# Loads of w_in and w_out issued by GpSimd instead of SyncE, in an attention and gated-MLP kernel on one core

## Chip, cores and metric

One Trainium2 chip, one of its cores. The metric is the device time of one execution of the kernel, in microseconds (us). The profile is one further execution, recorded by the hardware profiler.

## What is computed

An attention over 8 batches, 12 heads, 448 positions and 64 features, with a normalization of q and k, then a gated MLP with a residual. Cut to what matters:

```python
q_n, k_n = rmsnorm(q, g_q), rmsnorm(k, g_k)            # q, k, v: (8, 12, 448, 64) float32
scores = 1 / sqrt(64) * matmul(q_n, k_n.T)
attn = exp(scores - max(scores)); attn = attn / (sum(attn) + 1e-9)
x = matmul(attn, v)                                    # rearranged to (8, 448, 768)
h = gelu(x @ w_in)                                     # w_in: (768, 1024)
u, v = h[..., :512], h[..., 512:]
v_n = (v - mean(v)) / sqrt(var(v) + 1e-6) * g_ln
gated = u * (einsum('ts,bsd->btd', w_sg, v_n) + b_sg)  # w_sg: (448, 448)
return x + gated @ w_out                               # w_out: (512, 768)
```

`w_in` and `w_out` are stored as 64-bit floats. The kernel loads their raw words and builds 32-bit floats from them.

## The kernel before

**Two programs in one.** The text of the kernel writes down the work with engines bound to a `Tape` instead of the hardware: each call becomes a `Task` with an engine, a cost and a priority (its place in the text plus an offset). `Tape.schedule` then simulates the five engines and SyncE's DMA queue with the costs of `Tape.cost`, takes for each free engine the ready task of the best priority, and `Tape.emit` sends the instructions out in the order of the simulated begins. So the order on each engine is fixed when the kernel is built, and an engine runs its instructions in that order, each waiting for what it needs. All instructions sent by `emit` carry the line L439 in the profile, so groups are told apart by the names of tiles.

**The attention.** A unit is one pair of head pairs (24 units in all). For each, `load_qk` loads q and k into `qk`, `squares` and `norms` find the norms (`sqk`, `ss`, `nx`, `ny`), and `split` multiplies them in (on GpSimd, but for unit 0), cuts the result into two 16-bit halves `hl` and transposes these by DMA into `qt`. `scores` runs seven steps: matmuls `s`, a running minimum on VectorE (`jk`), the exponential on ScalarE (`ex`), a split into halves (`ahl`, on VectorE or ScalarE) and a DMA transpose into `at`. `pv` multiplies by v, takes reciprocals of the sums (`recips`, partly on GpSimd: `rx`, `rh`, `rl`) and writes the halves `xh` and `xl`.

**The weights.** `weights` is a generator that runs beside the first twelve steps of the attention. `load_raw` (L602 on) loads w_in in 12 pieces of 128 rows by 1024 words (`raw`, three buffers, `RAWB`); `decode` turns each into floats in five VectorE instructions (`dec`), and then ScalarE and VectorE write the two 16-bit parts `wi`. Further on come w_sg (`wsr`), transposed by DMA into `ws_h` and `ws_l`, and w_out in 8 pieces (`rawo`, L673 on), decoded the same way into `wr`. A piece's buffer is free for the next load when VectorE has read the last word of the piece in it. The first piece (`RAWF` = 1) may go at once; the others are held in the plan (`tape.after`) until the transposes of the first unit are out.

**Queues.** Every DMA, loads, stores and transposes alike, is issued by SyncE, in one queue, in the order of the plan. The plan models this queue: `schedule` keeps the time when the queue is empty, and the end of each SyncE DMA follows from it. A DMA on another engine has a fixed cost in the plan: `cost` returns 700 ns of issue and 4000 ns until the data is there.

**GpSimd and VectorE.** `Tape.port` says which tasks use the port to the on-chip memory that the two engines share: every GpSimd task, and VectorE's elementwise ones between tiles outside PSUM. The plan keeps them apart, and `emit` lets a GpSimd task of more than `LONG` (500 ns) wait for the VectorE port task sent before it.

**The MLP.** `moe` runs once per batch, interleaved with the attention of the next batches; its matmuls need the decoded weights.

Of the kernel before, what the change touches and what calls it, by code (L numbers as in the profile page):

```python
# [8 lines left out]
F32 = mybir.dt.float32  # L9
# [6 lines left out]
ALU = mybir.AluOpType  # L16
# [28 lines left out]
NQK, NVR, RAWB = 2, 2, 3  # L45
NAT, NAH, NQT, NVH, HLB, GV = 2, 3, 2, 4, 3, 3
NOT, NX, NEX = 2, 6, 2
EXP_SET = "natural_log_exp_and_others"
BACC_KW = dict(dynamic_dma_scratch_size=1024)
TILE_KW = dict()  # L50
# [53 lines left out]
class Tape:  # L104
# [30 lines left out]
    def cost(self, q, op, a, kw):  # L135

        aps = [x for x in kw.values() if isinstance(x, bass.AP)]
        n = max([self.free(x) for x in aps], default=1)
        wide = [k for k in ("in_", "in0", "in1") if k in kw and self.free(kw[k]) > max(n // 2, 1)]
        psum = any(self.tiles[kw[k].tensor.name].pool.space for k in wide if kw[k].tensor.name in self.tiles)  # L140
        if q.eng == "T":
            t, big = kw["lhsT"], kw["rhs"]
            rows, cols = (64 if ap_n <= 64 else 128 for ap_n in (t.shape[0], self.free(t)))
            m = self.free(big)
            d = max(m / 2.4, 26.7 if cols == 64 else 53)
            if big.dtype == F32R:
                d = max(d, 186)
            if big.dtype == F32:
                d = max(4 * m / 2.4, 250)
            return d * rows * cols / 128 ** 2 + (4 if rows == cols == 128 else 3), 170, (rows, cols)  # L150
        if q.eng != "S" and "dma" in op:
            return 700, 4000, None
        if q.eng == "S":
            b = n * kw["out"].shape[0] * mybir.dt.size(kw["out"].dtype)
            if "transpose" in op:
                return 1530, b / 458752, True
            return 600, b / 220e3, False
        if "preload" in op:
            return 1283, 0, None
        if q.eng == "A":  # L160
            ptr = sum(isinstance(kw.get(k), bass.AP) for k in ("bias", "scale"))
            return 0.833 * n + (52 if psum else 95) + 85 * ptr + (CA if "accum_out" in kw else 0), 100, None
        if q.eng == "V":
            if op == "reciprocal":
                return 70 + 6.5 * n, 75, None
            ptr = sum(isinstance(kw.get(k), bass.AP) for k in ("scalar", "scalar1", "scalar2"))
            one = len(wide) == 1 and not psum and "reduce" not in op and "bn" not in op and "accum_out" not in kw
            f32 = one and (mybir.dt.size(kw[wide[0]].dtype) == 4 or kw[wide[0]].dtype == U16)
            return (0.52 if f32 else 1.04) * n + 70 + 50 * ptr + (CV if "accum_out" in kw else 0), 85, None
        if n < 100:  # L170
            return 1.5 * n + 185, 20, None
        wide = [k for k in wide if len([x for x in kw[k].ap if x[0]]) == len(kw[k].ap)]
        return (1.86 if len(wide) > 1 else 2.5 if op == "tensor_scalar" else 1.64) * n + 210, 20, None
# [27 lines left out]
    def record(self, q, op, a, kw):  # L201
# [9 lines left out]
            t.id, t.off, t.key = len(self.tasks), self.off, key  # L211
            self.tasks.append(t)
        self.count += 1
        if q.eng == "S":
            t.preds |= self.after
        self.last = t if pe else None
        t.calls.append((q, op, a, kw))
# [229 lines left out]
def kernel(  # L447
# [74 lines left out]
    T, A, V, G, SP = (Queue(tape, e, x) for e, x in zip("TAVGS", (nc.tensor, nc.scalar, nc.vector, nc.gpsimd, nc.sync)))  # L522
    mm = T.matmul
    ENG = dict(A=A, V=V, G=G)

    def copy(out, in_, on):
        tape.either(*[(ENG[e], *(("activation", dict(out=out, in_=in_, func=AF.Copy)) if e == "A" else
# [9 lines left out]

    def two(out, in0, in1, op, on):
        tape.either(*[(ENG[e], "tensor_tensor", dict(out=out, in0=in0, in1=in1, op=op)) for e in on])

    SSW = 2 * C7

# [37 lines left out]
    def decode(dst, raw, most=None):  # L580

        hi, lo = raw[:, :, 1], raw[:, :, 0]
        di = dst.bitcast(I32)
        V.tensor_scalar(out=di, in0=hi, scalar1=0x7FFFFFFF, scalar2=None, op0=ALU.bitwise_and)
        more = {} if most is None else dict(op1=ALU.max, accum_out=most)
        V.tensor_scalar(out=dst, in0=dst, scalar1=LEAST, scalar2=None, op0=ALU.max, **more)
        V.tensor_scalar(out=di, in0=di, scalar1=3, scalar2=0x3FFFFFF8, op0=ALU.logical_shift_left, op1=ALU.bitwise_and)
        V.scalar_tensor_tensor(out=di, in0=hi, scalar=-0x40000000, in1=di, op0=ALU.bitwise_and, op1=ALU.bitwise_or)
        V.scalar_tensor_tensor(out=di, in0=lo, scalar=29, in1=di, op0=ALU.logical_shift_right, op1=ALU.bitwise_or)

    def weights():
        wi = const.tile([P, KT, 2, 2, DH], F16, name="wi")
# [9 lines left out]
        def load_raw(j):  # L602
            if j < len(chunks):
                x, t = chunks[j]
                held, tape.after = tape.after, set() if j < RAWF else tape.after
                raws[j] = stage.tile([P, DH, 2], I32, name="raw", bufs=RAWB)
                SP.dma_start(out=raws[j].rearrange("p a b -> p (a b)"),
                             in_=wi_b[t * P:(t + 1) * P, x * 2 * DH:(x + 1) * 2 * DH])
                tape.after = held

# [2 lines left out]
        for x in (1, 0):  # L613
# [13 lines left out]
            for t in range(KT):  # L627
                wh, wl = (wi[:, t, x, n] for n in range(2))
                A.activation(out=wh, in_=dec[t], func=AF.Copy, scale=wsc)
                V.scalar_tensor_tensor(out=wl, in0=dec[t], scalar=wsc, in1=wh, op0=ALU.mult, op1=ALU.subtract)  # L630
                if t % 2:
                    yield
            W["h", x], W["l", x] = wi[:, :, x, 0], wi[:, :, x, 1]
# [5 lines left out]

        wsr = [mlp.tile([P, S], F32, name="wsr", tag="ug", bufs=5) for c in range(CK)]  # L640
        for s_ in range(C7):
            SP.dma_start(out=wsr[s_ // 2][s_ % 2 * HP:(s_ % 2 + 1) * HP],
                              in_=w_sg.rearrange("(p c) s -> c p s", c=C7)[s_])
        spart = const.tile([P, CK], F32, name="ws_part")
        G.memset(out=spart, constant=0.0)
# [25 lines left out]
        for j in range(2 * FT):  # L671
            t, es = j // 2, slice(j % 2 * EH, (j % 2 + 1) * EH)
            raw = mlp.tile([P, EH, 2], I32, name="rawo", tag="v" + "hl"[j % 2])  # L673
            SP.dma_start(out=raw.rearrange("p a b -> p (a b)"),
                         in_=wo_b[t * P:(t + 1) * P, 2 * EH * (j % 2):2 * EH * (j % 2 + 1)])
            wr = mlp.tile([P, EH], F32, name="wr", tag="gt", bufs=NOT)
            decode(wr, raw)
# [22 lines left out]
    def load_qk(u, qs=None):  # L700
        if u >= NI // NG:
            return
        qs = qs or [SP]
        b, h0 = u // NU, u % NU * 2 * NG
        qk = ld.tile([P, 2, 2, C7, D], F32, name="qk", bufs=NQK)
        for x, src in enumerate((q, k)):
# [8 lines left out]
    def load_v(i):  # L715
# [7 lines left out]
        vp = vr.rearrange("p g c d -> p g (c d)")  # L723
        src = v[b, 2 * g:2 * (g + GV)].rearrange("(g h) (p c) d -> h p g (c d)", h=2, c=C7)
        for h, half, s0, c0, n in ((0, lo, 0, 0, C4), (0, hi, 0, C4, CM), (1, lo, C4, C4, CM), (1, hi, CM, 0, C4)):
            SP.dma_start(out=vp[half, :, s0 * D:(s0 + n) * D], in_=src[h][:, :, c0 * D:(c0 + n) * D])
        for j in range(GV):
            VR[i + j] = vp[:, j]

# [67 lines left out]
    def vsplit(i):  # L797
# [3 lines left out]
        vr = VR.pop(i)  # L801
        vf = vh.rearrange("p c d -> p (c d)")
        A.activation(out=vf, in_=vr, func=AF.Copy, scale=sc)
        V.scalar_tensor_tensor(out=vl.rearrange("p c d -> p (c d)"), in0=vr, scalar=sc, in1=vf, op0=ALU.mult, op1=ALU.subtract)
        r.update(vh=vh, vl=vl)

    GR = (slice(0, C4), slice(C4, C7))
# [49 lines left out]
    def rows(e, rh, rl):  # L857
# [6 lines left out]
                       rhs=ident_h, start=(t == 0 and rx is rh), stop=(t == n - 1 and rx is rl), skip_group_check=True)  # L864
        if ROWP:
            return ps
        row = att.tile([P, C4 * P], F32, name="row", bufs=1)[:, 0:n * P]
        scaled(row, ps, 2.0 ** -25, RW)
        return row

# [2 lines left out]
    def pv(u, e):  # L873
# [17 lines left out]
                yield  # L891
        if ROWP:
            row = rows(e, *r_)
        V.tensor_tensor(out=ps, in0=ps, in1=row, op=ALU.mult)
        if e == 0:
            U[u]["x"] = tuple(xp.tile([P, NG, C7, HP], F16, name="x" + c) for c in "hl")
        xh, xl = (x.rearrange("p j c q -> p c j q")[:, GR[e]] for x in U[u]["x"])
        ps = ps.rearrange("p (c j q) -> p c j q", j=NG, q=HP)
        copy(xh, ps, XH)
        V.tensor_tensor(out=xl, in0=ps, in1=xh, op=ALU.subtract)  # L900
        if e == 1:
            for j in range(NG):
                XT[NG * u + j] = tuple(x[:, j].rearrange("p c q -> p (c q)") for x in U[u]["x"])
# [16 lines left out]
    def moe(b, early=False):  # L920
# [151 lines left out]
        for t in range(CM + b % 2):  # L1072
# [26 lines left out]
                copy(ot[:, es], ps[:, 0:EH], OT)  # L1099
                yield  # L1100
            for h in range(2):
                SP.dma_start(out=om[b % 2, 2 * t + h] if t < CM else om[h, C7 - 1], in_=ot[h * HP:(h + 1) * HP])
        if b % 2 == 1:
            del GT[b - 1]
        for g in range(NP):
# [143 lines left out]
```

## Time and profile before

| | us |
|---|---|
| median of 3 runs | 860.91 |
| lowest, highest | 857.09, 862.02 |
| profiled execution, its own time | 860.37 |
| profiled execution, span | 858.6 |
| TensorE (PE) busy in the span | 743.0 |
| ScalarE (ACT) busy | 722.3 |
| VectorE (DVE) busy | 668.2 |
| GpSimd (POOL) busy | 304.5 |

The span runs from the first to the last recorded instruction; 1.8 us of the profiled execution lie around it. The mean granted TensorE clock was 0.936. In all views, times are in us from the span's start unless a column says ns; PEld is the load of weights into TensorE, SPq is SyncE issuing DMAs. A name such as `at<-ahl` means that `at` is written from `ahl`, with buffer numbers left out. In brackets stands for how long an engine was idle before an instruction, and what it waited for.

### The profile page before, as it was taken

The page shows a single profiled execution, that of the slowest core. Times are in us where ns is not written, and L with a number is a line of the kernel's source. Part 1 is how long each engine was busy: PE and PEld are TensorE (multiplying, and loading weights), DVE is VectorE, ACT ScalarE, POOL GpSimd, SP SyncE. Part 2 cuts the span into 40 slices and gives each one's busy share as a digit, 9 for nine tenths or more (in the row PEclk, how much of TensorE's full clock was granted, in tenths as well). Part 3 has the DMA queues.
Part 4 walks back from the last instruction along what each step waited for, and adds up shares of the span by engine and source line. Part 5 has one row for each costly group of instructions (what it writes and reads, how often), then busy time and mean ns, then how long its engine had stood idle before and what let it go on. Part 6 is the DMA issues. An engine that isn't in the chain of part 4 may idle for free.

```text
span 858.6 us, 21024 instructions
## 1 busy us (share of the span) xinstructions
PE 743.0 (87%) x7766; PEld 475.1 (55%) x7766; DVE 668.2 (78%) x1691; ACT 722.3 (84%) x1495; POOL 304.5 (35%) x457
## 2 busy tenths in 40 slices
PE   0445568954999979999999999999999999999997
PEld 0223343532675548655765568556855686558557
DVE  6978988889988878977976898878987978574250
ACT  4677879998898999898989999889999999895451
POOL 2543350045534634452444246323435335000000
PEclk9658668966999999999999999999999999999999
DMA  6999999969999998999699979997999699646002
GB/s 165 252 241 195 216 207 199 213 141 200 169 234 218 226 190 166 246 209 166 137 206 225 226 145 226 240 209 134 198 225 218 140 223 200 136 90 143 19 1 74
DMA packets 433944, 155.97 MB, mean 182 GB/s; under 512 B 402545, under 2 KB 427697, under 8 KB 433841
## 3 DMA queue, kind: packets, MB, share of 16 engines
q1 hardware_dynamic: 433840, 154.63, 89.6%
q8 instruction: 61, 1.00, 0.5%
q14 instruction: 43, 0.34, 0.1%
HBM read 43.57 MB, written 11.01 MB: 64 GB/s over the span
## 4 chain that ended last, share of the span: by engine, by line
PE 55%; ACT 17%; DVE 12%; DMA 9%; issue 5%; POOL 1%; SPq 1%; ACTq 0%; DVEq 0%; POOLq 0%
PE pv L439 11%; PE s L439 7%; DMA at<-ahl 6%; ACT ex L439 4%; ACT ahl L439 3%; DVE jk L439 2%; ACT L439 2%; ACT sqk L439 2%; PE row L439 1%; DVE ahl L439 1%; DMA qk<-in_k_dram 1%; ACT vg L439 1%; ACT u L439 1%; ACT vh L439 1%; DVE pv L439 1%
## 5 line engine op out<-in xcount | busy, mean ns | idle before, releaser
L439 DVE TENSOR_SCALAR_CACHE_REDUCE jk<-s 128x448 bf16<-128x448 f32 x336 | 199.0, 615 | 34.8 <-PE s L439 34.4
L439 ACT ACTIVATE ex<-s,nm 128x448 int32<-128x448 f32 x336 | 213.6, 641 | 12.1 <-DVE jk L439 9.8
L439 ACT ACTIVATE ahl<-ex 128x896 f16<-128x896 uint16 x192 | 181.9, 957 | 9.5 <-DMA at<-ahl 8.9
L439 PE MATMUL s<-qt 64*64 64x448 f16 x2016 | 142.8, 375 | 48.4 <-DMA qt<-hl 21.3
L439 PEld LDWEIGHTS <-vh 128*64 128x64 f16 (+2 forms) x1792 | 103.2, 112 | 103.6 <-issue 55.7
L439 PE MATMUL pv<-at,vh 128*64 128x192 f16 (+3 forms) x1536 | 133.0, 275 | 27.6 <-ACT ex L439 12.3
L439 DVE TENSOR_SCALAR ahl<-ex 128x896 f16<-128x896 uint16 x144 | 102.5, 712 | 28.8 <-ACT ex L439 22.7
L439 PEld LDWEIGHTS <-qt 64*64 64x64 f16 x2016 | 64.7, 110 | 94.4 <-issue 52.5
L439 POOL TENSOR_TENSOR hl<-qk,hl 128x896 f16<-128x896 f32 (+2 forms) x69 | 93.7, 1364 | 41.7 <-ACT hl L439 9.7
L439 PEld LDWEIGHTS <-wi 128*128 128x128 f16 x576 | 54.5, 99 | 55.5 <-issue 7.2
L439 POOL TENSOR_TENSOR qk<-qk,ny 128x896 f32<-128x896 f32 x46 | 77.1, 1690 | 14.5 <-DVE ahl L439 7.5
L439 POOL TENSOR_TENSOR qk<-qk,gg 128x896 f32<-128x896 f32 x23 | 48.1, 2093 | 96.0 <-ACT sqk L439 77.4
L439 PEld LDWEIGHTS <-xh 128*128 128x128 f16 (+1 forms) x648 | 49.7, 102 | 47.7 <-issue 20.8
L439 PE MATMUL pv<-at,vl 128*64 128x192 f16 (+3 forms) x768 | 74.0, 273 | 0.0
L439 ACT ACTIVATION_READ_ACCUMULATOR ex<-s,nm 128x1 f32 x336 | 71.6, 213 | 0.0
L439 POOL TENSOR_SCALAR rx<-sums 128x8 f32<-128x8 f32 (+1 forms) x48 | 15.0, 313 | 141.8 <-ACT ex L439 140.3
L439 PEld LDWEIGHTS <-vl 128*64 128x64 f16 (+2 forms) x896 | 56.1, 114 | 12.8 <-issue 0.7
L439 DVE TENSOR_REDUCE ss<-sqk 128x14 f32<-128x896 f32 x48 | 51.8, 1079 | 10.2 <-ACT sqk L439 10.1
L439 DVE TENSOR_TENSOR pv<-pv,row 128x512 f32<-128x512 f32 (+1 forms) x48 | 30.2, 629 | 34.3 <-PE pv L439 34.1
L439 ACT ACTIVATE sqk<-qk 128x896 f32<-128x896 f32 x48 | 45.8, 960 | 3.4 <-DMA qk<-in_k_dram 1.8
L439 PEld LDWEIGHTS <-xl 128*128 128x128 f16 (+1 forms) x408 | 36.6, 102 | 19.5 <-DVE v_i L439 1.1
L439 ACT ACTIVATE xh<-pv 128x512 f16<-128x512 f32 (+1 forms) x48 | 26.2, 547 | 24.4 <-DVE pv L439 23.7
(1104 smaller groups left out, 1799.7 us busy)
## 6 DMA issues: line engine op xcount, KB each, us to landing
qk<-in_q_dram SPq DMA_DIRECT2D x48, 224.0 KB, 3.9
qk<-in_k_dram SPq DMA_DIRECT2D x48, 224.0 KB, 4.7
out_dram<-ot SPq DMA_DIRECT2D x56, 192.0 KB, 3.4
raw<-in_moe_w_in_dram SPq DMA_DIRECT2D x12, 512.0 KB, 5.4
vr<-in_v_dram SPq DMA_DIRECT2D x32, 192.0 KB, 4.2
vr<-in_v_dram SPq DMA_DIRECT2D x32, 144.0 KB, 3.7
rawo<-in_moe_w_out_dram SPq DMA_DIRECT2D x8, 384.0 KB, 3.6
at<-ahl SPq DMA_TRANSPOSE x168, 4.6
```

What stands on the lines that cost most here:

```text
L439: ins = getattr(q.nc_eng, op)(*first, *a, **kw)
```

## The change

The loads of w_in (12) and w_out (8) are issued by GpSimd. A DMA on an engine other than SyncE costs 1100 ns of issue in the plan instead of 700, with the same 4000 ns until its data is there; no other DMA of the kernel is on such an engine. Tasks with a DMA on any engine are now held by `tape.after`, where only SyncE's were. The other new names choose engines that were fixed before and keep their values, so that they change nothing: VectorE for `DEC`, `XL`, `VL` and `WL`, SyncE for `SQ_`, `VQ`, `KQ` and `XQ`.

```diff
+DEC, XL, VL, WL = 'V', 'V', 'V', 'V'
+RQ, OQ, SQ_, VQ, GLAT, KQ, XQ = 'G', 'G', 'S', 'S', (1100, 4000), 'S', 'S'
...
         if q.eng != "S" and "dma" in op:
-            return 700, 4000, None
+            return *GLAT, None
...
-        if q.eng == "S":
+        if "dma" in op:
             t.preds |= self.after
...
+    LD = dict(S=SP, G=G, A=A)
...
                 raws[j] = stage.tile([P, DH, 2], I32, name="raw", bufs=RAWB)
-                SP.dma_start(out=raws[j].rearrange("p a b -> p (a b)"),
+                LD[RQ].dma_start(out=raws[j].rearrange("p a b -> p (a b)"),
                              in_=wi_b[t * P:(t + 1) * P, x * 2 * DH:(x + 1) * 2 * DH])
...
             raw = mlp.tile([P, EH, 2], I32, name="rawo", tag="v" + "hl"[j % 2])
-            SP.dma_start(out=raw.rearrange("p a b -> p (a b)"),
+            LD[OQ].dma_start(out=raw.rearrange("p a b -> p (a b)"),
                          in_=wo_b[t * P:(t + 1) * P, 2 * EH * (j % 2):2 * EH * (j % 2 + 1)])
```

More of the change, by code (lines that the diff above doesn't have):

```diff
@@ L539, in two, with stt @@
         tape.either(*[(ENG[e], "tensor_tensor", dict(out=out, in0=in0, in1=in1, op=op)) for e in on])
+    def stt(out, in0, by, in1, op0, op1, on):
+        tape.either(*[(ENG[e], "scalar_tensor_tensor", dict(out=out, in0=in0, scalar=by, in1=in1, op0=op0, op1=op1)) for e in on])
     SSW = 2 * C7
@@ L629, in weights @@
                 A.activation(out=wh, in_=dec[t], func=AF.Copy, scale=wsc)
-                V.scalar_tensor_tensor(out=wl, in0=dec[t], scalar=wsc, in1=wh, op0=ALU.mult, op1=ALU.subtract)
+                stt(wl, dec[t], wsc, wh, ALU.mult, ALU.subtract, WL)
                 if t % 2:
@@ L641, in weights @@
         for s_ in range(C7):
-            SP.dma_start(out=wsr[s_ // 2][s_ % 2 * HP:(s_ % 2 + 1) * HP],
+            LD[SQ_].dma_start(out=wsr[s_ // 2][s_ % 2 * HP:(s_ % 2 + 1) * HP],
                               in_=w_sg.rearrange("(p c) s -> c p s", c=C7)[s_])
@@ L702, in load_qk @@
             return
-        qs = qs or [SP]
+        qs = qs or [LD[KQ if u else "S"]]
         b, h0 = u // NU, u % NU * 2 * NG
@@ L725, in load_v @@
         for h, half, s0, c0, n in ((0, lo, 0, 0, C4), (0, hi, 0, C4, CM), (1, lo, C4, C4, CM), (1, hi, CM, 0, C4)):
-            SP.dma_start(out=vp[half, :, s0 * D:(s0 + n) * D], in_=src[h][:, :, c0 * D:(c0 + n) * D])
+            LD[VQ].dma_start(out=vp[half, :, s0 * D:(s0 + n) * D], in_=src[h][:, :, c0 * D:(c0 + n) * D])
         for j in range(GV):
@@ L803, in vsplit @@
         A.activation(out=vf, in_=vr, func=AF.Copy, scale=sc)
-        V.scalar_tensor_tensor(out=vl.rearrange("p c d -> p (c d)"), in0=vr, scalar=sc, in1=vf, op0=ALU.mult, op1=ALU.subtract)
+        stt(vl.rearrange("p c d -> p (c d)"), vr, sc, vf, ALU.mult, ALU.subtract, VL)
         r.update(vh=vh, vl=vl)
@@ L866, in rows @@
             return ps
-        row = att.tile([P, C4 * P], F32, name="row", bufs=1)[:, 0:n * P]
+        row = att.tile([P, C4 * P], F32, name="row", bufs=2 if "G" in XL else 1)[:, 0:n * P]
         scaled(row, ps, 2.0 ** -25, RW)
@@ L893, in pv @@
             row = rows(e, *r_)
-        V.tensor_tensor(out=ps, in0=ps, in1=row, op=ALU.mult)
+        if "G" in XL:
+            sx = att.tile([P, C4 * P], F32, name="sx", tag="row", bufs=2)[:, 0:n * P]
+            V.tensor_tensor(out=sx, in0=ps, in1=row, op=ALU.mult)
+            ps = sx
+        else:
+            V.tensor_tensor(out=ps, in0=ps, in1=row, op=ALU.mult)
         if e == 0:
@@ L899, in pv @@
         copy(xh, ps, XH)
-        V.tensor_tensor(out=xl, in0=ps, in1=xh, op=ALU.subtract)
+        two(xl, ps, xh, ALU.subtract, XL)
         if e == 1:
@@ L1101, in moe @@
             for h in range(2):
-                SP.dma_start(out=om[b % 2, 2 * t + h] if t < CM else om[h, C7 - 1], in_=ot[h * HP:(h + 1) * HP])
+                LD[XQ if b < B - 1 else "S"].dma_start(out=om[b % 2, 2 * t + h] if t < CM else om[h, C7 - 1], in_=ot[h * HP:(h + 1) * HP])
         if b % 2 == 1:
```

2 lines of the change are left out of this document (1 added, 1 removed).

## The prediction

> **What bounds the kernel now.** I read the page first, then the sums over stretches of time, then the chain that ended last, and last the timelines of SyncE's queue (SPq), VectorE (DVE) and GpSimd (POOL). The sums over stretches say where time can move at all; columns are the stretch, its length, then busy time and count of PE, PEld, DVE, ACT and POOL, the granted TensorE clock, DMA share and GB/s.
>
> ```profile
> span 858.6 us, 21024 instructions
> ...
> 0.00:25.00 25.00, 3.74 (x45) 2.50 (x49) 15.62 (x28) 11.44 (x20) 8.39 (x24) 1.00 0.70 178
> 25.00:50.00 25.00, 9.05 (x86) 3.80 (x78) 23.36 (x57) 16.87 (x34) 11.75 (x14) 0.56 1.12 230
> 50.00:75.00 25.00, 10.00 (x126) 7.21 (x128) 19.79 (x54) 21.82 (x46) 9.81 (x11) 0.70 1.09 230
> 75.00:100.00 25.00, 16.29 (x160) 10.12 (x158) 23.03 (x45) 19.46 (x37) 13.20 (x15) 0.64 1.14 219
> 100.00:125.00 25.00, 15.12 (x180) 8.49 (x174) 24.20 (x65) 16.41 (x33) 8.49 (x12) 0.77 0.98 210
> 125.00:150.00 25.00, 20.85 (x192) 10.39 (x191) 19.16 (x60) 23.15 (x49) 2.88 (x5) 0.82 0.93 197
> 150.00:175.00 25.00, 22.63 (x212) 12.19 (x210) 22.25 (x68) 24.79 (x48) 1.80 (x6) 1.00 0.91 198
> 175.00:200.00 25.00, 9.66 (x108) 5.82 (x107) 21.95 (x51) 23.66 (x49) 14.93 (x21) 0.64 0.75 165
> ...
> 600.00:700.00 100.00, 98.03 (x1092) 65.23 (x1085) 85.24 (x223) 94.92 (x205) 43.30 (x64) 1.00 1.01 199
> ```
>
> The reader is to see two kernels in one. Late, TensorE is busy 98.03 of 100 us, so nothing that loads weights matters there. Early, it is mostly idle: from 25 to 125 us DVE leads with 23.36 + 19.79 + 23.03 + 24.20 = 90.4 of 100 us, and from 125 to 200 us ACT leads with 71.6 of 75. All twenty loads that the change moves lie in this early part. Its ceiling follows: no more than 100 - 90.4 = 9.6 us of DVE idle and 75 - 71.6 = 3.4 us of ACT idle can go, **13.0 us** together. What is gained there shifts the TensorE-bound rest forward whole.
>
> The page's DMA queues and issues (KB each, median us from issue to landing) show that one queue carries everything:
>
> ```profile
> q1 hardware_dynamic: 433840, 154.63, 89.6%
> ...
> raw<-in_moe_w_in_dram SPq DMA_DIRECT2D x12, 512.0 KB, 5.4
> ...
> rawo<-in_moe_w_out_dram SPq DMA_DIRECT2D x8, 384.0 KB, 3.6
> at<-ahl SPq DMA_TRANSPOSE x168, 4.6
> ...
> qt<-hl SPq DMA_TRANSPOSE x48, 4.4
> ```
>
> The transposes `at<-ahl` feed the attention's matmuls, and loads of `raw` stand in the same line. The chain that ended last (start, us, what) and SPq's timeline show where one stands behind the other:
>
> ```profile
> 2.88 4.61 DMA qk<-in_k_dram
> ...
> 29.43 6.32 DMA qt<-hl
> ...
> 40.21 7.41 DMA at<-ahl
> ...
> 65.63 7.83 DMA at<-ahl
> ```
>
> ```profile
> 7.23 0.59 SPq L439 DMA_DIRECT2D raw<-in_moe_w_in_dram  x1
> 15.63 3.28 SPq L439 DMA_TRANSPOSE qt<-hl  x2
> ...
> 26.81 1.54 SPq L439 DMA_DIRECT2D raw<-in_moe_w_in_dram  x3
> ...
> 29.43 8.07 SPq L439 DMA_TRANSPOSE qt<-hl  x2
> ...
> 47.34 0.54 SPq L439 DMA_DIRECT2D raw<-in_moe_w_in_dram  x1
> ...
> 49.59 1.24 SPq L439 DMA_DIRECT2D raw<-in_moe_w_in_dram  x1
> ...
> 62.07 3.50 SPq L439 DMA_DIRECT2D raw<-in_moe_w_in_dram  x2
> 65.63 2.28 SPq L439 DMA_TRANSPOSE at<-ahl  x1
> ...
> 98.06 2.13 SPq L439 DMA_DIRECT2D raw<-in_moe_w_in_dram  x2
> ```
>
> Three loads (1.5 MB) go out at 26.81 us just before the pair of `qt` transposes at 29.43, whose issue then takes 8.07 us where the pair at 15.63 took 3.28. Two loads go out at 62.07 just before the transpose at 65.63, which lands after 7.83 us instead of the median 4.6.
>
> **The change part by part.** *Removed from SPq.* The issues, and the waits that stood before them (us in total, times, longest):
>
> ```profile
> L439 SPq DMA_DIRECT2D raw<-in_moe_w_in_dram x12: 327/532/1240, 7.2 to 99.9; - x12
> ```
>
> ```profile
> SPq L439 <- DVE dec L439: 6.0, 5, 2.6
> SPq L439 <- DVE wr L439: 5.4, 5, 1.9
> ```
>
> Twelve issues of 0.53 us (6.4 us) leave SPq, eight more for w_out, and 11.4 us of waiting for DVE to free a buffer. I count these at nothing: the chain enters SPq hardly at all here, since the transposes at 29.43 and 65.63 go out as soon as their data is ready. What counts is the line behind them: the chain's transposes would land in their median time. 6.32 - 4.4 = 1.9 us, 7.41 - 4.6 = 2.8 us (the one at 40.21 stands behind the `qt` pair that took 8.07 us) and 7.83 - 4.6 = 3.2 us: **7.9 us gained**. The bounds are 0, if the bytes are in the way from another queue too, and the 13.0 us ceiling. I take the whole 7.9, because DVE comes to the two loads of 62.07 us only later (its next first read of a `raw`, from its timeline, stands below), so nothing is late next if transposes overtake them.
>
> ```profile
> 81.61 0.38 DVE L439 TENSOR_SCALAR dec<-raw 128x512 int32<-128x512 int32 x1
> ```
>
> The Trainium skill, "DMA: Bandwidth & Descriptors", section "Issuing engines are not separate DMA queues", speaks against this: DMAs from any engine share the same 16 engines and interleave, and a second issuer saves only the time to issue. By that rule the 7.9 us would be about 0; with its one queue, this trace cannot test it.
>
> *Moved forward in time.* The first w_in load leaves SPq's seventh place and goes out on POOL next to the first q and k loads, whose landing (4.61 us at 2.88) starts everything. Its 0.5 MB at the 230 GB/s of the second row above are 2.2 us of DMA time: bounds 0 and 2.2 us on the path, and I take the middle, **1.1 us lost**, since it collides with part of the q and k loads only.
>
> *Added on POOL.* Twenty issues, which no row shows. The nearest rows are SPq's 0.33 us from below and POOL's longest instruction from above:
>
> ```profile
> 19.33 2.07 POOL L439 TENSOR_TENSOR qk<-qk,gg 128x896 f32<-128x896 f32 x1 [7.37 <-DVE dec L439]
> ```
> I take 1.1 us, between the two, which the plan now counts as well: 22 us in 200 where POOL is busy for 71. POOL is in order, so behind each issue wait the `qk` and `hl` pieces and the small reciprocals; `hl` feeds the `qt` transposes, and TensorE waits for those. POOL's idle time (129 of 200 us) hides it; without that cover, each issue standing ahead of a late `hl` would cost 1.1 us. The plan treats an issue on POOL as a user of the port that it shares with DVE, and `emit` makes it wait for the DVE instruction planned before it. What sharing costs DVE now:
>
> ```profile
> L439 DVE SCALAR_TENSOR_TENSOR dec<-raw,dec x24: 678/690/1701, 17.8 to 114.7; 128x512 int32<-128x512 int32 x24
> ```
>
> ```profile
> L439 DVE SCALAR_TENSOR_TENSOR dec<-raw,dec 128x512 int32<-128x512 int32 x22 | 17.5, 804 | 0.0
> ```
>
> One decode step takes 678 ns undisturbed, 1701 at worst beside POOL, 804 on average between 25 and 200 us. So one issue costs DVE 0 to 1.0 us; from the average I take 0.13 us, for the twelve w_in loads **1.5 us lost** (at worst 12 us). The eight w_out loads fall where ACT leads with 24.79 of 25 us, so theirs is hidden; without that cover it is another 1 us (8 at worst).
>
> *The order.* Every engine's order is written anew by the plan, with w_in's bytes no longer in its model of SPq's queue. I put the shift at 0; it can go either way, and the run-to-run spread of before (857.09 to 862.02) is no measure of it.
>
> **Sum** against the profiled execution's own 860.37 us (span 858.6): 860.37 - 7.9 + 1.1 + 1.5 = 855.1, **855 us**. The median of three is 860.91, so this is 0.7% below it. Half a per cent (4.3 us) is about what a measurement of this kernel can tell from no change.
>
> **Rivals.** *A, the bytes are in the way from any queue: no change.* For it: DMA share is 1.09 to 1.14 from 25 to 100 us, the engines have no free time, and `raw` comes in rows of 4 KB, so in turns with short transpose packets it still goes first. Against it: an engine with two queues has something to move while a short packet is underway. Then the first term falls away: 860.4 + 1.1 + 1.5 = 863.0, within 0.5%.
>
> *B, DVE waits for w_in behind POOL: slower.* Now some loads are read almost as they land:
>
> ```profile
> 52.91 0.41 DVE L439 TENSOR_SCALAR dec<-raw 128x512 int32<-128x512 int32 x1
> ...
> 55.65 0.99 DVE L439 TENSOR_SCALAR dec<-raw 128x512 int32<-128x512 int32 x1 [0.30 <-DMA raw<-in_moe_w_in_dram]
> ...
> 104.52 0.42 DVE L439 TENSOR_SCALAR dec<-raw 128x512 int32<-128x512 int32 x1
> ```
>
> ```profile
> 48.41 3.33 POOL L439 TENSOR_TENSOR qk<-qk,ny 128x896 f32<-128x896 f32 x2 [1.44 <-DVE ahl L439]
> 53.12 4.30 POOL L439 TENSOR_TENSOR hl<-qk,hl 128x896 f16<-128x896 f32 x3 [1.37 <-ACT hl L439]
> ```
>
> Loads issued at 47.34, 49.59 and 98.06 us are read 5.6, 6.1 and 6.5 us later, against a median landing of 5.4. On POOL such an issue meets runs of 3.3 and 4.3 us, half of which (1.9) it waits on average, plus 0.6 for its longer issue: 2.5 us late. DVE is in order, so three such loads cost 7.5 us, of which nothing comes back where DVE leads: 860.4 + 7.5 = 868, with no gain. It decides once a load is over about 1 us later than now. Against it: the plan places the issue where POOL is free, and only 0.3 us of waiting for `raw` is seen today. The Trainium skill, "SBUF — State Buffer", section "Who interferes with whom", supports B: a DMA from GpSimd stalls while a two-port VectorE instruction keeps GpSimd from writing its descriptors. No row here has such a DMA.
>
> **How the numbers follow.** Forecast 0.42 (847 to 856.6; the end below is the 13.0 us ceiling), A 0.30 (856.6 to 865.2), B 0.28 (865.2 to about 874.5, the worst DVE price of 12 us and 2.2 us at the start). Chances: faster by over 0.5% 0.42, within 0.30, slower 0.28. The range drops a tenth at each end: 847 to 871.
>
> **What would show it.** Right: a second queue with 6.3 + 3.1 MB; chain pieces `at<-ahl` under 5 us between 25 and 125 us; DVE idle below 9.6 us there; TensorE done with the early part sooner, and the same 98 of 100 us late. A: pieces still 7 us long, DVE as before. B: DVE waiting for `raw` over 5 us in total, or POOL waiting for DVE ahead of its issues with `hl` late behind them. The forecast is wrong at its root if the early part is paced by something no load touches, such as the ACT and DVE work itself in the new order.

## The result, and the profile after

The changed kernel takes **867.71 us** in the median of 14 runs (863.03 to 875.91); the kernel before, 860.91 in 14 runs (857.09 to 864.65). The ratio is **1.0091**, 95% interval 1.0068 to 1.0114 (it lies by the quotient of the means, 1.0090; that of the medians is 1.0079): slower by about 0.9%, where 0.7% faster was forecast. Nine of the 14 runs lie between 863.0 and 868.6, five between 872.2 and 875.9. The profiled execution, 872.23 us, is one of the upper five, which has to be kept in mind in reading it. Runs more than 1.5% above the fastest of the same kernel count for no ratio; among the experiments this concerns two of the nine runs of `e6`.

The page of the changed kernel: DMA queues (packets, MB, share of the time of the 16 DMA engines) and issues (KB each, median us from issue to landing).

```profile
q1 hardware_dynamic: 430960, 145.19, 83.1%
q0 software_dynamic: 2368, 9.44, 4.1%
...
raw<-in_moe_w_in_dram POOLq DMA_DIRECT2D x12, 512.0 KB, 6.7
...
rawo<-in_moe_w_out_dram POOLq DMA_DIRECT2D x8, 384.0 KB, 4.8
at<-ahl SPq DMA_TRANSPOSE x168, 4.4
```

The second queue is there, with the 9.44 MB of the twenty loads. Each load takes longer from issue to landing than it did from SyncE: 6.7 us in place of 5.4, and 4.8 in place of 3.6. The transposes, which were to gain by it, went from 4.6 to 4.4.

The sums over stretches of the changed kernel (stretch, length, busy time and count of PE, PEld, DVE, ACT and POOL, granted clock, DMA share, GB/s):

```profile
0.00:25.00 25.00, 0.00 (x0) 0.12 (x1) 13.96 (x18) 9.74 (x15) 10.22 (x25) 1.00 0.57 135
25.00:50.00 25.00, 10.80 (x102) 5.68 (x101) 19.16 (x47) 16.79 (x34) 12.39 (x13) 0.68 1.11 254
50.00:75.00 25.00, 8.92 (x90) 5.69 (x94) 12.77 (x36) 12.80 (x26) 6.21 (x10) 0.57 1.11 165
...
600.00:700.00 100.00, 99.54 (x1087) 63.95 (x1086) 86.14 (x212) 94.50 (x204) 44.80 (x63) 1.00 0.95 190
```

Late, TensorE is busy 99.54 of 100 us, as good as before, so most of the loss is to be looked for elsewhere. Early, two rows stand out. In the first 25 us TensorE does not begin (it did 45 matmuls before). From 50 to 75 us DVE falls from 19.79 to 12.77 and ACT from 21.82 to 12.80 us, while the DMA share is 1.11 after 1.09 but the bytes fall from 230 to 165 GB/s: the DMA engines are as occupied as before and move less. (The share adds up the time of all packets under way on the 16 engines, so it can pass 1.)

The start, in the timeline of the changed kernel:

```profile
1.53 0.72 POOL L441 DMA_DIRECT2D raw<-in_moe_w_in_dram  x1
...
19.68 3.33 SPq L441 DMA_TRANSPOSE qt<-hl  x2
...
25.26 2.08 PE L441 MATMUL s<-qt 64*64 64x448 f16 x20 [25.26 <-DMA qt<-hl]
```

The first w_in piece leaves GpSimd at 1.53 us, where SyncE sent it at 7.23. The first pair of `qt` transposes goes out at 19.68 instead of 15.63. TensorE starts at 25.26; before, at 21.26.

The stretch around 60 us, from the same kernel's timeline:

```profile
50.03 18.43 SPq L441 DMA_TRANSPOSE at<-ahl  x3
50.28 0.57 POOL L441 DMA_DIRECT2D raw<-in_moe_w_in_dram  x1 [2.32 <-DVE v_x L441]
...
65.81 0.43 DVE L441 TENSOR_SCALAR dec<-raw 128x512 int32<-128x512 int32 x1 [6.32 <-DMA raw<-in_moe_w_in_dram]
...
66.29 1.79 ACT L441 ACTIVATE ahl<-ex 128x896 f16<-128x896 uint16 x2 [7.99 <-DMA at<-ahl]
```

and two sums of 2.5 us in it:

```profile
60.00:62.50 2.50, 0.00 (x0) 0.00 (x0) 0.00 (x0) 0.00 (x0) 0.17 (x1) 0.50 1.10 80
62.50:65.00 2.50, 0.00 (x0) 0.00 (x0) 0.00 (x0) 0.00 (x0) 0.00 (x0) 0.50 1.44 80
```

A load goes out on GpSimd at 50.28, in the middle of SyncE's transposes. VectorE reads it at 65.81, 15.5 us later, and ScalarE, which needs a buffer that a transpose empties, goes on at 66.29. From 60 to 65 us hardly any engine works, and the DMA engines move 80 GB/s at a share of 1.10 to 1.44. Neither transfer has overtaken the other: both are late.

**Theories.** *Theory 1, the collision:* loads of a second queue and transposes of SyncE's queue, in flight together, slow each other, beyond what their bytes explain. *Theory 2, the plan:* loads from GpSimd land later than the 4.0 us that the plan counts, so work is placed too early and its engine waits. *Rivals to both:* the new order is a worse one whatever the queue; the shared port costs it; GpSimd, which now stands at its issues, is late with its own work.

### The profile page after: what moved, and what is told of

Its sections match the earlier page's. It is cut to its first block, busy times and chain, and to the rows that moved or that the text cites. A ratio compares the mean times of both kernels' runs of the same rounds, so it can differ in the third digit from the quotient of the medians.

```text
span 870.5 us, 21057 instructions
## 1 busy us (share of the span) xinstructions
PE 747.7 (86%) x7766; PEld 475.9 (55%) x7766; DVE 672.2 (77%) x1701; ACT 714.9 (82%) x1484; POOL 328.4 (38%) x478
## 3 DMA queue, kind: packets, MB, share of 16 engines
q0 software_dynamic: 2368, 9.44, 4.1%
## 4 chain that ended last, share of the span: by engine, by line
PE 49%; ACT 21%; DVE 14%; DMA 6%; issue 6%; SPq 1%; POOL 1%; ACTq 0%; DVEq 0%; POOLq 0%
PE pv L441 10%; PE s L441 6%; ACT ex L441 6%; ACT ahl L441 4%; DVE jk L441 3%; ACT L441 2%; DMA at<-ahl 2%; DVE dec L441 2%; DMA vr<-in_v_dram 2%; PE row L441 2%; SPq L441 1%; ACT vg L441 1%; DVE ahl L441 1%; ACT sqk L441 1%; DVE ss L441 1%
## 5 line engine op out<-in xcount | busy, mean ns | idle before, releaser
L441 PE MATMUL s<-qt 64*64 64x448 f16 x2016 | 146.7, 381 | 50.9 <-DMA qt<-hl 27.2
L441 ACT ACTIVATE ahl<-ex 128x896 f16<-128x896 uint16 x187 | 177.8, 959 | 12.1 <-DMA at<-ahl 11.5
L441 DVE TENSOR_SCALAR ahl<-ex 128x896 f16<-128x896 uint16 x149 | 106.3, 714 | 27.3 <-ACT ex L441 21.7
L441 POOL TENSOR_TENSOR hl<-qk,hl 128x384 f16<-128x384 f32 (+2 forms) x69 | 94.7, 1379 | 38.6 <-DVE hl L441 13.4
L441 POOL TENSOR_TENSOR qk<-qk,gg 128x896 f32<-128x896 f32 x24 | 50.1, 2088 | 100.6 <-ACT sqk L441 70.9
L441 POOL TENSOR_SCALAR rx<-sums 128x8 f32<-128x8 f32 (+1 forms) x48 | 20.7, 431 | 112.3 <-ACT ex L441 110.3
```

Of the source, the lines that this page charges most:

```text
L441: ins = getattr(q.nc_eng, op)(*first, *a, **kw)
```

## The experiments

In the edits, `Queue(tape, "S", nc.gpsimd)` is a queue that the plan treats as SyncE's while the instruction goes to GpSimd, and `Queue(tape, "G", nc.sync)` is the reverse. With these, the order of the work on PE, VectorE, ScalarE and GpSimd stays as planned, and only the engine that issues the loads differs.

**1. The order or the queue: `e1_order_before_queue_after` and `e2_order_after_queue_before`.** The kernel before, with the twenty loads sent by GpSimd:

```diff
-    ENG = dict(A=A, V=V, G=G)
+    ENG, GD = dict(A=A, V=V, G=G), Queue(tape, "S", nc.gpsimd)
...
-                SP.dma_start(out=raws[j].rearrange("p a b -> p (a b)"),
+                GD.dma_start(out=raws[j].rearrange("p a b -> p (a b)"),
...
-            SP.dma_start(out=raw.rearrange("p a b -> p (a b)"),
+            GD.dma_start(out=raw.rearrange("p a b -> p (a b)"),
```

> The order of before on TensorE, VectorE and ScalarE, unchanged; only the twenty loads are issued by GpSimd, at the places in time that the old plan gave them. Theory 1 (two queues): 863 to 872, with loads or transposes landing after over 10 us between 25 and 80 us. Theory 2 (the order): 860 within 2. Theory 3 (GpSimd late behind its issues): 863 to 868, with hl and the qt transposes later, but no slow landings.

The change, with the twenty loads sent by SyncE and no wait for the shared port before them:

```diff
-                elif t.port and holder is not None and t.occ > LONG:
+                elif t.port and holder is not None and t.occ > LONG and "dma" not in op:
...
-    LD = dict(S=SP, G=G, A=A)
+    LD = dict(S=SP, G=Queue(tape, "G", nc.sync), A=A)
```

> The order of after on TensorE, VectorE and ScalarE, unchanged; the twenty loads go back to SyncE at the places that the new plan gave them, and the wait of a load for the shared port is dropped. Theory 1: 861 to 865, at most the 4 us that the first transposes are later (19.7 against 15.6 us), and no stall near 57 to 66 us. Theory 2: 866 to 869, as the change itself.

Measured: `e1` 880.96 us, ratio 1.0219 [1.0199, 1.0239]; `e2` 861.77, ratio 1.0006 [0.9992, 1.002]. The new order costs nothing that can be measured. The whole loss, 867.7 - 861.8 = 5.9 us, comes with GpSimd as the issuing engine. In the old order, made for loads from SyncE, this costs 19 us, more than any theory had named; the new plan, which knows that GpSimd issues, avoids 13 of them.

`e2` and the changed kernel differ in who sends the loads, and in the wait for the port, which experiment 5 weighs by itself. They do not tell a second queue from a GpSimd that stands at its issues; the transfers speak for the queue. Transfers from 50 to 75 us (KB each, median us to landing), in `e2`:

```profile
DMA packets 9818, 4.74 MB, mean 190 GB/s; under 512 B 8918, under 2 KB 9430, under 8 KB 9816
...
raw<-in_moe_w_in_dram SPq DMA_DIRECT2D x3, 512.0 KB, 4.8
...
at<-ahl SPq DMA_TRANSPOSE x4, 6.2
```

and in the changed kernel:

```profile
DMA packets 8262, 4.13 MB, mean 165 GB/s; under 512 B 7420, under 2 KB 7928, under 8 KB 8260
...
raw<-in_moe_w_in_dram POOLq DMA_DIRECT2D x2, 512.0 KB, 14.0
...
at<-ahl SPq DMA_TRANSPOSE x4, 11.2
```

The same transposes take 11.2 us instead of 6.2, beside loads that take 14.0 instead of 4.8.

**2. The queues alone: `e0_queues_alone`.** No kernel, only its DMAs: in each stretch, six transposes of the kernel's size (T) on SyncE, six w_in loads (L), or both in turns, and VectorE reading each result.

```python
    for _ in range(2):
        section("T", None)
        section("L", nc.sync)
        section("L", nc.gpsimd)
        section("TL", nc.sync)
        section("TL", nc.gpsimd)
        section("TL", nc.scalar)
```

> Leaves out the whole computation: six stretches, done twice, of 6 transposes (128x1792, 16 bit) and 6 loads (512 KB) alone. Stretches: transposes alone; loads alone from SyncE; loads alone from GpSimd; both in turn in SyncE's queue; transposes from SyncE with loads from GpSimd; transposes from SyncE with loads from ScalarE. Theory 1 (two queues disturb each other): with loads from GpSimd the twelve take over 1.3 times as long as in one queue, and a transpose lands after 8 us or more where one alone takes 4 to 5. Theory 2 (only the order of the plan): the same total within 10% from one queue or two.

The first results read in three stretches, from VectorE's timeline of the first pass (start, us, in brackets the idle time before and what ended it). The stretches begin at 42.7 us (one queue), 66 (loads by GpSimd) and 88.5 (loads by ScalarE):

```profile
46.62 0.15 DVE L57 CAST tok<-at 128x1 f32<-128x1 f16 x1 [3.83 <-DMA at<-src]
...
65.67 0.15 DVE L59 CAST tok<-raw 128x1 f32<-128x1 int32 x1 [1.23 <-DMA raw<-in_moe_w_in_dram]
73.57 0.15 DVE L57 CAST tok<-at 128x1 f32<-128x1 f16 x1 [7.46 <-DMA at<-src]
...
80.11 0.15 DVE L57 CAST tok<-at 128x1 f32<-128x1 f16 x1 [6.28 <-DMA at<-src]
...
106.00 0.15 DVE L57 CAST tok<-at 128x1 f32<-128x1 f16 x1 [17.42 <-DMA at<-src]
...
120.92 0.15 DVE L59 CAST tok<-raw 128x1 f32<-128x1 int32 x1
```

Alone, six transposes take 15 us, six loads 12 from SyncE and 13 from GpSimd. Six of each in one queue take 23 us, and the first transpose is there after 3.83. With the loads on GpSimd the whole took 22 us in this pass and 27 in the second, the first transpose 7.5 and 10.1, the second one 14 and 19. With the loads on ScalarE it was 33 and 31 us, and 17.4 for the first transpose. So a second queue hardly shortens the whole in its best case, lengthens it by 5 to 10 us in the other three, and delays the first transposes in all four. A part of this delay is plain sharing: GpSimd sends its six loads within 4 us, so the first transposes meet all of them, where in one queue loads and transposes take turns. The factor of 1.3 that the collision was to show held for ScalarE (1.4) and not for GpSimd (0.96 and 1.2); the lateness of transposes held for both.

**3. The start: `e3_first_on_sync` and `e8_order_e3_all_sync`.** The change with the first w_in piece on SyncE, planned so; and the order of that with all loads on SyncE, by the edit of `e2`.

```diff
-                LD[RQ].dma_start(out=raws[j].rearrange("p a b -> p (a b)"),
+                LD["S" if j == 0 else RQ].dma_start(out=raws[j].rearrange("p a b -> p (a b)"),
```

> As the change, but the first piece of w_in is issued by SyncE. If the later start (first q and k transposes at 19.7 us against 15.6) comes from the first piece going early: they are back at 15 to 17 us and the time is 863 to 865. If only the queues matter (theory 1): 866 to 869 as the change, or a start that is no earlier.

> The order of e3 (new plan, first piece on SyncE) on TensorE, VectorE and ScalarE, unchanged; all twenty loads issued by SyncE at the places that this plan gave them, without the wait for the shared port. Theory 1 (a second queue delays transposes and loads): 857 to 861, faster than e3's 863.2. Theory 2 (only order and start count): 863 within 1.5, as e3.

Measured: `e3` 863.17, ratio 1.0025 [1.0007, 1.0043]; `e8` 860.83, 0.9995 [0.9983, 1.0007]. The transposes of the first unit go out at 15.44 us again and TensorE starts at 20.95. With one load of twenty on SyncE, and the order planned for it, 4.5 us of the 6.8 are gone; the other nineteen loads still cost 2.3 in this order.

**4. Parts of the loads, in the order of before: `e4_order_before_w_in_2_to_12` and `e5_order_before_w_out`.** As `e1`, with only w_in's later eleven pieces, or only w_out's eight, sent by GpSimd.

```diff
-                GD.dma_start(out=raws[j].rearrange("p a b -> p (a b)"),
+                (GD if j else SP).dma_start(out=raws[j].rearrange("p a b -> p (a b)"),
```

> The order of before on TensorE, VectorE and ScalarE; eleven of the twelve w_in loads issued by GpSimd, the first one and w_out's by SyncE. Theory 1: 868 to 874, most of the 19 us of e1, as these loads fall among the densest transposes. If w_out's loads carry e1's loss: 861 to 864. The start is as in before (first q and k transposes at 15.6 us).

> The order of before on TensorE, VectorE and ScalarE; only the eight w_out loads issued by GpSimd. Theory 1: 861 to 865, as the transposes are sparser there (DMA share 0.75 to 0.93) and ScalarE leads. If it is VectorE waiting for loads that land late behind GpSimd (rival B of the prediction): 866 to 872, with VectorE waiting over 5 us for rawo.

Measured: `e4` 867.04, ratio 1.008 [1.0049, 1.011]; `e5` 867.8, 1.0072 [1.0054, 1.0089]. In an order that has no room for it, either part costs 6 to 7 us by itself; `e4` lies below the 868 that theory 1 had as its least. How w_out's costs it, in the timeline of `e5`:

```profile
151.80 1.28 POOL L439 DMA_DIRECT2D rawo<-in_moe_w_out_dram  x2 [0.49 <-issue]
157.68 0.36 DVE L439 TENSOR_SCALAR wr<-rawo 128x384 int32<-128x384 int32 x1 [4.72 <-DMA rawo<-in_moe_w_out_dram]
...
161.15 0.69 POOL L439 DMA_DIRECT2D rawo<-in_moe_w_out_dram  x1 [8.06 <-DVE wr L439]
```

and in the kernel before:

```profile
150.16 0.58 SPq L439 DMA_DIRECT2D rawo<-in_moe_w_out_dram  x1
...
153.86 0.35 DVE L439 TENSOR_SCALAR wr<-rawo 128x384 int32<-128x384 int32 x1
```

The first load goes out 1.6 us later and is read 5.9 us after its issue instead of 3.7; VectorE stands 4.72 us. The third issue then stands 8.06 us on GpSimd until VectorE has freed a buffer. That is rival B of the prediction, a load read almost as it lands, shown here for w_out in the old order. Theory 1's 861 to 865 for `e5` was a miss.

**5. The shared port: `e6_no_port_wait`.** The change in its own order, without the wait of a load for VectorE's instruction on the shared port (the first edit of `e2`).

> As the change, same order on every engine, but a load on GpSimd no longer waits for the VectorE instruction planned before it on the shared port. If that wait makes the loads late: 862 to 865. If not (theory 1): 866 to 870, as the change.

Measured: 873.51 us in the median of all nine runs (863.2 to 877.9), ratio 1.0112 [1.0077, 1.0147]. That wait is not the loss: without it nothing is gained. The time lies above what either reading had named.

**6. The price in the plan: `e7_measured_price`, `e11_price_alone`, `e12_order_e7_all_sync`.** `e7` is `e3` with the measured price of a GpSimd load in the plan; `e11` is `e7` with the first piece on GpSimd, all else in the same order but for VectorE's decoding of this piece, which the plan puts earlier; `e12` is the order of `e7` with all loads on SyncE.

```diff
-RQ, OQ, SQ_, VQ, GLAT, KQ, XQ = 'G', 'G', 'S', 'S', (1100, 4000), 'S', 'S'
+RQ, OQ, SQ_, VQ, GLAT, KQ, XQ = 'G', 'G', 'S', 'S', (600, 6700), 'S', 'S'
```

> The change with the first w_in piece issued by SP, and the plan given the measured price of a GpSimd load: 0.6 us of issue and 6.7 us to landing, in place of 1.1 and 4.0. With the plan's old price and the first piece on SP the time was 863.2, and the same order with all loads on SP 860.8. Theory 2 (what is left, 2.3 us, is work placed too early for loads that land later than the plan counts): 859 to 862, VectorE's waits for raw and rawo under 2 us in all. Theory 1 (what is left is the landing of transposes and loads in flight together, which no price in the plan alters): 862 to 866, the landings as before, raw 6 us in the median and some above 10.

> The change with one edit: the plan counts 0.6 us of issue and 6.7 us to landing for a GpSimd load, in place of 1.1 and 4.0; the first w_in piece stays on GpSimd, so that on every engine the order is that of e7_measured_price (860.1) but for this one load. Theory 2 (two losses that add: the start, and loads that the plan counts on too early): the start's loss stays, the first matmul comes 3 to 4 us later than in e7, and the time is 863 to 866, with VectorE's waits for raw and rawo under 2 us in all. Theory 1 (the collision in flight, which no price alters): 866 to 870, as the change. Third (the start costs nothing once the rest is planned right): 859 to 862.

> The order of e7_measured_price (860.1) on PE, VectorE, ScalarE and GpSimd, with the twenty loads issued by SP. If a queue of their own still costs something in an order that has room for it (theory 1): 855 to 858, faster than e7 and than the kernel before. If, with room in the plan, the queue costs nothing (theory 2): 859 to 862, with no difference that 3 rounds show. If SP's queue holds loads up behind transposes in this order, which asks for them earlier than SP is free: 862 to 866, and e7 would owe its time to the queue of their own.

Measured: `e7` **860.08**, ratio 0.9996 [0.9975, 1.0016]; `e11` 864.12, 1.004 [1.0022, 1.0058]; `e12` 861.8, 1.0002 [0.9982, 1.0022]. In `e7`, as theory 2 had it, the loss is gone, VectorE waits for neither `raw` nor `rawo`, and yet the landings are as long as before (`raw` 6.9 us in the median). In this order the queue costs nothing that can be measured. TensorE's first matmuls in `e7`:

```profile
20.80 5.74 PE L441 MATMUL s<-qt 64*64 64x448 f16 x62 [20.80 <-DMA qt<-hl]
```

and in `e11`:

```profile
23.91 5.33 PE L441 MATMUL s<-qt 64*64 64x448 f16 x62 [23.91 <-DMA qt<-hl]
```

The two kernels differ in one load and its decoding. Together they start TensorE 3.1 us later and cost 864.1 - 860.1 = 4.0 us in time. Most of it is the load: VectorE's second sum `ss`, ahead of which no decoding stands, comes 2.6 us later (10.95 after 8.31 us). This is the cleanest measure of the start.

**7. Which figure of the price, and a collision caught: `e13_landing_alone`, `e14_issue_alone`, `e15_order_e13_all_sync`, `e16_e13_w_in_5_to_7_sync`.** `e3` with (1100, 6700) and with (600, 4000) in the plan; the order of `e13` with all loads on SyncE; and `e13` in its order with three loads on SyncE, which then do not wait for the port either:

```diff
-                LD["S" if j == 0 else RQ].dma_start(out=raws[j].rearrange("p a b -> p (a b)"),
+                LD["S" if j == 0 else "X" if j in (4, 5, 6) else RQ].dma_start(out=raws[j].rearrange("p a b -> p (a b)"),
```

where `X` is `Queue(tape, "G", nc.sync)`.

> First w_in piece on SP; of the plan's price only the landing is the measured one, 6.7 us in place of 4.0; the issue stays 1.1. With both old it was 863.2, with both measured 860.1. Theory 2 (the early landing does the harm): 859 to 862 and no waits of VectorE for raw or rawo over 2 us in all. If the issue's price does it: 862 to 865, as with the old price.

> First w_in piece on SP; of the plan's price only the issue is the measured one, 0.6 us in place of 1.1; the landing stays 4.0. Theory 2: 862 to 865 with VectorE waiting 3 us or more for raw and rawo, as with the old price (863.2). If the issue's price is what matters: 859 to 862.

> The order of e13_landing_alone (872.4 us, with engines standing from about 54 to 60 us while w_in loads and transposes are in flight) on PE, VectorE, ScalarE and GpSimd, with all loads issued by SP. Theory 1 (the loss is the second queue's loads landing together with SP's transposes): 859 to 863, no such hole, raw landing 6 us in the median. Rival (e13's order is a poor one in itself): 868 to 873.

> e13_landing_alone (872.4 us) in the same order on PE, VectorE, ScalarE and GpSimd, with three of its twenty loads, the w_in pieces 5 to 7 that GpSimd issued at 43, 46 and 53 us into the flight of five transposes, issued by SP, and all others as in e13. Theory 1 (the collision of these three with the transposes is the loss): 861 to 866, the hole before 60 us gone. If the loss is spread over all loads of the second queue: 868 to 872.

Measured: `e13` **872.39**, ratio 1.0129 [1.0105, 1.0154]; `e14` 862.94, 1.0026 [0.9997, 1.0054]; `e15` 865.67, 1.0058 [1.0041, 1.0075]; `e16` 868.24, 1.0088 [1.0056, 1.0119]. A right landing in the plan by itself made it worse, against theory 2: any new figure gives a new order, and with it other loads meet other transposes. `e13` against `e15` shows such a meeting with the order kept. Sums of 2.5 us in `e13`:

```profile
52.50:55.00 2.50, 0.00 (x0) 0.00 (x0) 1.33 (x5) 0.00 (x0) 0.87 (x2) 0.50 1.38 112
55.00:57.50 2.50, 0.00 (x0) 0.00 (x0) 0.00 (x0) 0.00 (x0) 0.00 (x0) 0.50 1.45 78
57.50:60.00 2.50, 0.00 (x0) 0.00 (x0) 0.00 (x0) 0.00 (x0) 0.00 (x0) 0.50 0.95 162
```

and in `e15`:

```profile
52.50:55.00 2.50, 0.00 (x0) 0.00 (x0) 1.38 (x5) 1.49 (x4) 0.24 (x1) 0.50 1.18 300
55.00:57.50 2.50, 0.50 (x6) 0.43 (x8) 2.24 (x6) 2.50 (x6) 1.08 (x2) 0.50 1.25 267
57.50:60.00 2.50, 2.50 (x26) 1.83 (x24) 1.45 (x2) 2.50 (x5) 1.87 (x2) 0.50 0.97 188
```

With loads on GpSimd all engines stand for 5 us at 78 and 162 GB/s; with all loads on SyncE the DMA engines move 267 and 188 GB/s in these stretches, and the engines work. The transfers of 50 to 62.5 us in `e13`:

```profile
raw<-in_moe_w_in_dram POOLq DMA_DIRECT2D x1, 512.0 KB, 10.7
at<-ahl SPq DMA_TRANSPOSE x2, 10.3
```

and in `e15`:

```profile
raw<-in_moe_w_in_dram SPq DMA_DIRECT2D x2, 512.0 KB, 5.0
at<-ahl SPq DMA_TRANSPOSE x5, 5.9
```

So 6.7 us of `e13`'s loss are the queue (872.4 - 865.7), and another 4.9 the order itself (865.7 against 860.8 of before), which neither theory had foreseen. Three loads sent by SyncE take back 4.2 (`e16`), but the intervals of `e13` and `e16` touch, and 868.2 lies where the loss was to lie if it is spread over all loads. In the profiled run of `e16` the standstill is gone (234 and 214 GB/s from 55 to 60 us): the three loads make the standstill, and not the whole loss.

**8. The same three loads in the change, and the change again: `e17_change_w_in_5_to_7_sync`, `e9_change_look_a`, `e10_change_look_b`.** The change in its order with the w_in pieces 5 to 7 on SyncE, as in `e16`; and the change unaltered, twice.

> The change (867.7 us, 863 to 876 in two groups) in the same order, with the w_in pieces 5 to 7, which GpSimd issued at 47, 50 and 58 us, issued by SP, and all others by GpSimd, the first included. Theory 1: the upper group is gone and the median is 862 to 865, of which the start, 3 to 4 us late, is what is left. If the collision of these three is no more than chance of the profiled run: 866 to 869, with two groups as before.

> The change itself, looked at once more, unaltered. Its timed runs lie in two groups, 863 to 869 us (9 runs) and 872 to 876 (5 runs), and the one profiled so far, 872.2, is of the upper group and has a hole of some 8 us from 57.5 to 65.8 us in which no engine works and the last transposes and w_in loads in flight land after 11 and 14 us. Theory 1 (the hole is the collision of loads in a second queue with SP's transposes, and comes or not from run to run): a look of the lower group has no such hole, the longest landing of w_in under 10 us, and is shorter by about the length of the hole, 6 to 9 us; its remaining loss stands at the start, where the first matmul comes 4 us later than before the change. Rival (the two groups differ elsewhere, by the granted clock): the hole is there in both, and the busy time of PE in the fixed work after 600 us differs.

> The same kernel a second time, as a second draw from the two groups: with the hole at 57 to 66 us at 872 to 876 us, without it at 863 to 869.

Measured: `e17` 866.76, ratio 1.0068 [1.0045, 1.0091], its eight runs from 863.7 to 870.6: not distinguishable from the change (1.0091), and above the 862 to 865 of theory 1. `e9` 870.47 and `e10` 871.14 us. `e9` has the hole again (62.5 to 65 us without any work, 124 GB/s). `e10` does not have it, and is as slow; there theory 1's reading of the two groups fell. Where `e10` loses instead, in sums over long stretches of `e10`:

```profile
125.00:250.00 125.00, 93.71 (x911) 54.34 (x912) 111.49 (x295) 109.91 (x226) 50.70 (x76) 0.84 0.91 192
...
400.00:600.00 200.00, 191.99 (x2059) 122.93 (x2056) 163.78 (x414) 178.96 (x377) 82.60 (x116) 0.99 0.97 195
```

and of `e2`, the same order with all loads on SyncE:

```profile
125.00:250.00 125.00, 97.40 (x974) 55.85 (x975) 113.09 (x302) 111.59 (x230) 45.81 (x67) 0.85 0.87 193
...
400.00:600.00 200.00, 194.00 (x2099) 124.25 (x2097) 167.03 (x419) 182.88 (x387) 86.62 (x120) 1.00 0.98 194
```

TensorE works 3.7 us less from 125 to 250 us, and 2.0 less from 400 to 600, where none of the twenty loads is in flight any more. In this late part one halt stands out in `e10`, from TensorE's timeline and in a sum of 2.5 us:

```profile
444.76 0.37 PE L441 MATMUL pv<-at,vh 64*64 64x192 f16 x2 [2.10 <-DMA at<-ahl]
```

```profile
445.00:447.50 2.50, 2.50 (x17) 2.22 (x14) 0.63 (x1) 2.42 (x8) 1.67 (x5) 0.50 1.27 287
```

TensorE stands 2.10 us for a transpose, and behind that its granted clock is 0.50 instead of 1.00. Over this halt `e10` falls from 5.6 to 9.0 us behind `e2`: VectorE, whose order is the same in both, begins its `ahl` before it at 445.27 and 439.68 us, and its `pv` behind it at 450.44 and 441.48. The profiled runs of the change, of `e9` and of `e6` have one such halt each (1.8 to 2.2 us before a `pv` at 446, 582 and 404 us, with the clock at 0.50 behind it); in `e2` and `e17` the clock is 1.00 all the way from 220 to 850 us. Why TensorE comes to stand there, and what makes the two groups of run times, stays open. The clock over the whole run, the rival put on record with `e9`, is 0.935 to 0.937 in the upper five runs and 0.935 to 0.943 in the other nine; as halts lower it too, this does not tell cause from effect.

The pairs with one order, in us (the kernel before had medians between 860.2 and 861.9 beside these runs, so that 1 us between two rows means nothing):

| order of | loads on SyncE | loads on GpSimd | difference |
|---|---|---|---|
| before | 861.9 (in the same runs) | 881.0 (`e1`) | +19.0 |
| the change | 861.8 (`e2`) | 867.7 | +5.9 |
| `e13`, first piece on SyncE | 865.7 (`e15`) | 872.4 | +6.7 |
| `e3`, first piece on SyncE | 860.8 (`e8`) | 863.2 | +2.3 |
| `e7`, first piece on SyncE | 861.8 (`e12`) | 860.1 | -1.7, within the intervals |

The second queue never gained a time that can be measured. What it costs is set by the order it meets. No version tried beats the kernel before.

## Why the prediction was wrong

**Where time can move: right in the main.** From 600 to 700 us TensorE kept its 99 of 100 us, and in the profiled run most of the loss lies in the stretches that the prediction named; but some 3 us came later, where nothing was to change.

**"The chain's transposes would land in their median time: 7.9 us gained": the step that failed.** It was held that a transpose is late because loads stand ahead of it in SyncE's line, so that without them it goes at once. From 25 to 50 us transposes did land sooner. Transfers there, in the kernel before:

```profile
at<-ahl SPq DMA_TRANSPOSE x3, 5.9
qt<-hl SPq DMA_TRANSPOSE x2, 6.8
```

and in the changed kernel:

```profile
at<-ahl SPq DMA_TRANSPOSE x3, 4.1
qt<-hl SPq DMA_TRANSPOSE x2, 4.9
```

and in `e2`, the new order with all loads still in SyncE's line:

```profile
at<-ahl SPq DMA_TRANSPOSE x3, 3.7
qt<-hl SPq DMA_TRANSPOSE x2, 5.0
```

So the sooner landing came with the new order, and not with the loads leaving the line. Nor are the loads away: they are in flight at the same time, and where they met transposes, as from 50 to 75 us, these took 11.2 us and the loads 14.0. "Nothing is late next if transposes overtake them" was the wrong choice: both came late, and VectorE's idle time from 25 to 125 us, which was to fall below 9.6 us, rose to 25. `e2` and `e15`, each with its order kept, show that this goes with loads issued by GpSimd; `e0` shows late transposes with nothing but DMAs running. The Trainium skill, "DMA: Bandwidth & Descriptors", section "Issuing engines are not separate DMA queues", says that a second issuer saves only the time to issue. On the missing gain the runs agree (`e7` against `e12`: 860.1 and 861.8, no difference that can be measured). Of the loss, 5.9 and 6.7 us in one order, it says nothing.

**"The first w_in load moved forward: 1.1 us lost", bounds 0 to 2.2: right in kind, mis-sized.** It is up to 4.0 us (`e11` against `e7`, decoding included), with TensorE 3.1 us later. The price was taken from its bytes at the mean bandwidth, and halved because only part of the q and k loads was to be hit; but six of the first eight land 1.5 to 3.0 us later in the change, and they lose more than that share: in `e1`, with this load beside them, the k load of 2.89 us landed after 7.59 us instead of 4.61.

**"Added on POOL", 1.1 us of issue each:** measured 0.61 us (w_in) and 0.57 us (w_out) in the median. **The port, 1.5 us lost:** not seen. The decode step that the term was taken from averages 789 ns from 25 to 200 us, after 804 before, and `e6` takes the wait away and gains nothing. The Trainium skill, "SBUF — State Buffer", section "Who interferes with whom", has a DMA from GpSimd stall beside a two-port VectorE instruction; no run here shows that this is the loss.

**"The order: 0":** right for this order (`e2`, 0.06% [-0.08, 0.2]). That was luck as much as judgement: the orders of `e13` and `e3` lie 4.8 us apart with every load on SyncE (865.7 and 860.8).

**Rival A** had it that nothing is gained, and named 863.0; the gain is indeed missing, but it had no place for a loss by the meeting. **Rival B** named 868, and DVE's waits for `raw` are 7.4 us in the profiled run, over the 5 that it asked for. Yet it was to come from loads that GpSimd issues late; here the load was issued in the middle of the transposes and landed 15.5 us later, and in `e10` DVE waits 1.0 us for `raw` with the time as long. Its other sign, POOL waiting for DVE ahead of its issues, was there too: 8.18 us before the third w_out load. It cost little, since VectorE is 8.6 us behind `e2` at its first read of w_out and 7.5 at the third. The number of B was met, its mechanism shown only for w_out in the old order (`e5`).

The accounting of the 6.8 us: in another order with the first piece on SyncE 4.5 of them are gone (`e3`), and in a third order, with the measured price in the plan as well, all (`e7`). How the 5.9 us in the change's own order divide can be read from two profiled runs, since VectorE's order is the same in `e2` and in the change. Its first `jk` begins 1.2 us later in the change (26.62 and 25.44 us), its first read of w_in's seventh piece 5.5 us later (92.41 and 86.92), of w_out's last piece 7.4 us later (190.58 and 183.23), and the span is 10.3 us longer. So in this run about 1 us is the start, 4 the meeting around 60 us, 2 lie between that and 190 us, and 3 behind it. In `e10`, which has no standstill at 60 us, the same marks are 0.8, -0.3, 3.6 and 9.2 us: the division is another in each run. And `e2` too starts late (TensorE at 24.07) and yet is as fast as before.

## What to carry to other kernels

A transfer that is late behind others in one queue was not freed here by a queue of its own: ask what it will be in flight with, and price that from a run in which both queues are busy, not from its median when it travels alone. Keep a load that is not urgent away from the first loads that everything waits for; one such load at the head of an idle queue, with its decoding, cost 4 us here. And where a plan writes the order, give each version its own plan and compare issuing engines within one order, since a changed price alone moved the time by up to 9 us (`e13` against `e3`).

## What the runs showed of the hardware

With transposes from SyncE and loads from another engine in flight, the DMA engines were recorded at a share of 0.95 to 1.45 and moved 78 to 162 GB/s, where one queue moved 188 to 300 in the same place of the same order (`e13`, `e15`). With nothing but DMAs running (`e0`), the delay was larger with the loads on ScalarE (first transpose 17.4 us) than on GpSimd (7.5 and 10.1), against 3.8 in one queue. A GpSimd load took 0.57 to 0.61 us to issue in the median, and in one order (the change against `e2`) landed 1.6 us (w_in, 6.7 after 5.1) and 0.9 us (w_out, 4.8 after 3.9) later than one from SyncE. TensorE, after standing 1.8 to 2.2 us late in the kernel, was granted half its clock for about 3.4 us (`e10` and three more profiled runs). Why the share stays full while the bytes fall was not found.
